# Moving and spreading a row scaling between ScalarE and GpSimd, and zero matmuls ahead of the first data, in a linear-attention and mixture-of-experts kernel

## The chip, the cores and the metric

The kernel runs on one core of a Trainium2 chip. A core has five engines with queues of their own, each of which starts its instructions in order: TensorE (PE, matrix products; the trace lists its weight loads apart, as PEld), VectorE (DVE), ScalarE (ACT), GpSimd (POOL) and SyncE (SP, here only for issuing transfers). They wait for each other by semaphores. SBUF is the on-chip memory of 128 partitions, PSUM the eight banks that TensorE writes its products to, and DMA engines move data from and to HBM. The metric is the device time of one launch in microseconds.

## What is computed

The reference runs a linear attention with an exponential feature map over 8 batches and 8 heads of 576 positions, then routes the 4608 resulting rows of 512 values to 8 experts with weights P found by 8 rounds of row and column normalisation:

```python
def phi(x):
    proj = np.einsum('bhsd,df->bhsf', x, w_phi)
    proj = proj - np.max(np.abs(proj), axis=-1, keepdims=True)
    return np.concatenate([np.exp(proj), np.exp(-proj)], axis=-1)
...
num = np.einsum('bhsf,bhfd->bhsd', q_p, kv)
den = np.einsum('bhsf,bhf->bhs', q_p, z)[..., None] + 1e-06
...
for e in range(E):
    h = np.maximum(x @ w1[e], 0.0)
    ye = h @ w2[e]
    out += P[:, e:e + 1] * ye
```

Each expert has a product up from 512 to 1024 and a product down to 512. The output of expert e is scaled row by row with column e of P and added up.

## The kernel before

**Order.** The program does not give instructions to the engines as it goes. It first writes a list of operations (`plan.op`, through the helpers `pe`, `act`, `dve`, `pool` and `dma`), each with its engine, an estimated duration, what it reads and writes (keys), and the buffers that it takes. `Plan.schedule` then plays the list through: at each step it takes the operation that can start earliest, on whichever engine, and among several that can start at the same time the one written first. That gives every engine's order. On the chip only the order within an engine and the true dependences remain; the estimated times do not. Estimates that matter below: TensorE columns / 2400 + 0.0025 us, ScalarE columns / 1200 + 0.09 us, VectorE columns / 960 + 0.09 us, GpSimd 0.00164 us for each unit of its given size + 0.17 us; a result reaches another engine 0.22 to 0.32 us after that. Operations marked `shared` (all of `pool`, and VectorE's sums through `sub`) are planned so that only one of them runs at a time on the two engines together.

**Start.** Transfers of the first k, q and v tiles go out on SP's queue (`load_qk`, `load_v`, lines 811 to 828), w_phi in two halves on the queues of ScalarE and GpSimd (line 813). VectorE meanwhile fills small tiles (lines 818, 833, 835) and casts w_phi (line 820). The first matrix work is the transposes of k and q (line 545, `pair_a`), whose results VectorE and ScalarE copy out (lines 549, 553); then come products with w_phi (recorded at line 468, the helper `mm`), maxima on VectorE (line 460) and exponentials on ScalarE (line 464).

**Attention and the first expert.** The string `order` at line 873 lists the steps of attention by hand, with the first expert's products (`up0`, `down0`) for the first groups among them. Rows come in nine groups g of 512. `down0` puts the first expert's output unscaled into `acc[g]`, a float32 tile of 128 x 4 x 512, since P isn't known yet: ScalarE copies two of the four row blocks (line 795), VectorE the others (line 802). `routing` computes P in a chain of small VectorE operations and TensorE products (lines 929 to 945) while the first expert's last groups are multiplied. P ends with line 945.

**Experts 1 to 7.** For each expert, `load_w` transfers the weights from GpSimd's queue (line 362), `sums_w` builds eight sums of weight quarters on VectorE (line 986), and nine loops over g run the seven products of Strassen's method in both directions, interleaved by the string `ORDER` (line 1282): the up products of group g (`up7`) with the down products of the group before it (`down7`, the entries X1, Y1, Z1, X2, X3, Z2, X4). All these products are recorded at line 1078. In `up7` ScalarE copies a bank out to U (line 1106) or applies the relu (line 1115), and VectorE adds U to another bank (line 1110). A bank is added to further only after it has been copied. In `down7` VectorE first makes four sums of hT (line 986). The results go to `acc[g]` in two ways: `read2` scales a bank with P on ScalarE (line 1230) and adds it on GpSimd (line 1233); `read` does both on VectorE (line 1218).

**The scaling of the first expert's output.** When `down7` is called for expert 1, it writes four operations for its group, ahead of the group's products (lines 1238 to 1243): `acc[g]` times column 0 of P, in place, on ScalarE. They need P, the first expert's output in `acc[g]`, and nothing else; so all 36 can start as soon as P and those outputs are there. Both kinds of additions to `acc[g]` in expert 1 wait for them.

Of the kernel before, what the change touches and what calls it, by code (L numbers as in the profile page):

```python
# [12 lines left out]
ALU = mybir.AluOpType  # L13
ACT = mybir.ActivationFunctionType
# [214 lines left out]
def kernel(  # L229
# [11 lines left out]
    nc = tc.nc  # L241
# [3 lines left out]
    N, DD = out.shape  # L245
# [22 lines left out]
    xT = const.tile([128, NP, N], BF16, name="xT")  # L268
    L = const.tile([128, NT, E], FP32, name="L")
    P = const.tile([128, NT, E], FP32, name="P")  # L270

    NA = 5
    acc = [accp.tile([128, 4, DD], FP32, name=f"acc{g}", tag=f"acc{g}") for g in range(NA)]
# [17 lines left out]
    def pe(cols, fn, r=(), w=(), takes=()):  # L291
        plan.op("PE", max(cols / 2400.0 + 0.0025, 0.032), 0.32, fn, r, w, takes)

    def act(el, fn, r=(), w=()):
        plan.op("ACT", el / 1200.0 + 0.09, 0.22, fn, r, w)

    def dve(el, fn, r=(), w=(), shared=False):
        plan.op("DVE", el / 960.0 + 0.09, 0.22, fn, r, w, shared=shared)

    def pool(el, fn, r=(), w=()):  # L300
        plan.op("POOL", el * 1.64e-3 + 0.17, 0.25, fn, r, w, shared=True)

    def dma(queue, nbytes, rate, fn, r=(), w=()):

        plan.op(queue, 0.8 if queue == "POOL" else 0.6, 0.0, fn, r, w, (), nbytes / rate / (125 / 100))
# [45 lines left out]
    def new(tag):  # L351
        return banks.new(int(tag[1])) if tag in ("P1", "P2") else R[tag].new()
# [29 lines left out]
    def load_qk(b, hh, nh, t, r=()):  # L382

        o = hh % 4
        keys = [o // 2] if nh == 2 else [0, 1]
        if b < 2:
            g = t["f"]
            for x, src in ((1, k), (0, q)):
                i = 2 * x + o // 2
                dma("SP", nh << 17, 268, lambda x=x, src=src, i=i: nc.sync.dma_start(  # L390
                    out=acc[g][:, i:i + nh // 2].rearrange("p a (h c) -> p (a h) c", h=2),
                    in_=src[b, hh:hh + nh, 0:SM].rearrange("h (p j) d -> p h (j d)", j=NJ)),
                    r, [("acc", g, 2 * x + n) for n in keys])
            return
        for x, src in ((1, k), (0, q)):
            dma("POOL", nh << 17, 200, lambda x=x, src=src: nc.gpsimd.dma_start(
                out=t["qk"]()[:, x, o:o + nh],
                in_=src[b, hh:hh + nh, 0:SM].rearrange("h (p j) d -> p h (j d)", j=NJ)),
                r, [(t["qk"], x, i) for i in keys])
# [25 lines left out]
    def new_half(b, i):  # L425

        t = {"T": new("qkT"), "v": new("v_m")}
        if b < 2:
            return {"f": 4 - 2 * b - i, **t}
        return {"qk": new("qk"), **t}  # L430
# [36 lines left out]
    def mm(out_, lhsT, rhs, start, stop):  # L467
        nc.tensor.matmul(out_, lhsT=lhsT, rhs=rhs, start=start, stop=stop)  # L468
# [310 lines left out]
    def akey(g):  # L779
        return ["late"] * (g >= NA) + ["P"] * (g >= 9)  # L780
# [27 lines left out]
    for b in range(2):  # L808
        for i in range(2):
            halves[b, i] = new_half(b, i)  # L810
    load_qk(0, 0, 2, halves[0, 0])
    for i, (queue, eng) in enumerate((("ACT", nc.scalar), ("POOL", nc.gpsimd))):
        dma(queue, 1 << 15, 100, lambda i=i, eng=eng: eng.dma_start(
            out=wphi_f[64 * i:64 * i + 64, :], in_=w_phi), w=[f"wphi_f{i}"])
# [4 lines left out]
    for i in range(2):  # L819
        dve(64, lambda i=i: nc.vector.tensor_copy(  # L820
            out=wphi2[64 * i:64 * i + 64, i, :], in_=wphi_f[64 * i:64 * i + 64, :]),
# [4 lines left out]
    for h0 in (4, 6):  # L826
# [3 lines left out]
        out=wgate, in_=moe_w_gate.rearrange("(c p) e -> p c e", p=128)), w=["wgate"])  # L830
    for i in range(2):
        for x in range(2):
            dve(300, lambda i=i, x=x: nc.vector.memset(vrd[i][x], 0.0),
                w=[("vrd", i, x, h, *y) for h in range(2) for y in ((), (1,))])
# [338 lines left out]
    def down7(e, g, hT, B7):  # L1173


        def a(i, j):
            return lambda: hT[j]()[:, :, 256 * i:256 * i + 256]

        def hk(i, j):
            return [(hT[j], fp, i) for fp in range(2)]  # L1180

        late, seen = akey(g), set()
        S = [new("S") for _ in range(4)]
        S01 = dve
        sub(dve, 1024, lambda: S[2](), a(0, 0), a(1, 0), ALU.subtract, hk(0, 0) + hk(1, 0),
            [S[2]])
        sub(S01, 1024, lambda: S[0](), a(1, 0), a(1, 1), ALU.add, hk(1, 0) + hk(1, 1), [S[0]])
        sub(S01, 1024, lambda: S[1](), lambda: S[0](), a(0, 0), ALU.subtract,
            [S[0]] + hk(0, 0), [S[1]])
        sub(dve, 1024, lambda: S[3](), a(0, 1), lambda: S[1](), ALU.subtract,  # L1190
            [S[1]] + hk(0, 1), [S[3]])

        def prod(bank, lhs, y, r, first, more=()):
            f, r2 = B7[y]
            product(bank, lambda k, i: lhs()[:, k, 128 * i:128 * i + 128],
                    lambda k: f()[:, k, :], 4, r + r2 + (["P"] if e else late) + list(more), first)

        def start(bank, i, j):

            out_ = acc_part(g, i, j)  # L1200
            w = [("acc", g, 2 * i + n, j) for n in range(2)]
            if (i, j) in seen:
                dve(500, lambda: nc.vector.tensor_tensor(
                    out=out_(), in0=bank().rearrange("p (a b) -> p a b", a=2), in1=out_(),
                    op=ALU.add), [bank] + late, w)
            else:
                act(512, lambda: nc.scalar.copy(
                    out=out_(), in_=bank().rearrange("p (a b) -> p a b", a=2)),
                    [bank] + late, w)
            seen.add((i, j))  # L1210

        def read(bank, i, j):

            if e == 0:
                return start(bank, i, j)
            for n in range(2):
                ts = 2 * i + n
                dve(330, lambda n=n, ts=ts: nc.vector.scalar_tensor_tensor(  # L1218
                    out=acc[g][:, ts, 256 * j:256 * j + 256],
                    in0=bank()[:, 256 * n:256 * n + 256], scalar=P[:, 4 * g + ts, e:e + 1],  # L1220
                    in1=acc[g][:, ts, 256 * j:256 * j + 256], op0=ALU.mult, op1=ALU.add),
                    [bank, "P"], [("acc", g, ts, j)])

        def read2(bank, i, j):

            if e == 0:
                return start(bank, i, j)
            u = new("V")
            for n in range(2):
                act(390, lambda n=n: nc.scalar.activation(  # L1230
                    out=u()[:, n, :], in_=bank()[:, 256 * n:256 * n + 256], func=ACT.Copy,
                    bias=0.0, scale=P[:, 4 * g + 2 * i + n, e:e + 1]), [bank, "P"], [(u, n)])
            pool(670, lambda: nc.gpsimd.tensor_tensor(  # L1233
                out=acc[g][:, 2 * i:2 * i + 2, 256 * j:256 * j + 256],
                in0=acc[g][:, 2 * i:2 * i + 2, 256 * j:256 * j + 256], in1=u(), op=ALU.add),
                [(u, 0), (u, 1)], [("acc", g, 2 * i + n, j) for n in range(2)])

        if e == 1 and g < 9:
            for ts in range(4):
                act(512, lambda ts=ts: nc.scalar.activation(  # L1240
                    out=acc[g][:, ts, :], in_=acc[g][:, ts, :], func=ACT.Copy, bias=0.0,
                    scale=P[:, 4 * g + ts, 0:1]), ["P", ("acc", g, ts)] + akey(g),
                    [("acc", g, ts, j) for j in range(2)])
        x, y, z = new("P1"), new("P1"), new("P1")

        def X1():
            prod(x, a(0, 0), "11", hk(0, 0), True, S[1:3])
            read2(x, 0, 0)

        def Y1():  # L1250
            prod(y, a(0, 1), "21", hk(0, 1), True)
            read2(y, 0, 0)

        def Z1():
            prod(z, lambda: S[0](), "t1", [S[0]], True, S[3:4])
            read2(z, 1, 1)

        def X2():
            prod(x, lambda: S[1](), "t2", [S[1]], False)
            read(x, 0, 1)  # L1260

        def X3():
            prod(x, lambda: S[2](), "t3", [S[2]], False)
            read2(x, 1, 1)

        def Z2():
            prod(z, lambda: S[3](), "22", [S[3]], False)
            read(z, 0, 1)

        def X4():  # L1270
            prod(x, a(1, 1), "t4", hk(1, 1), False)
            read(x, 1, 0)

        def stores():
            if e == E - 1:
                for ts in range(4):
                    store(g, ts)

        return {"out": stores, "X1": X1, "Y1": Y1, "Z1": Z1, "X2": X2, "X3": X3, "Z2": Z2, "X4": X4}
# [56 lines left out]
```

## Time and profile before

| | |
|---|---|
| median of 3 runs | 1036.67 us (1035.63 to 1037.01) |
| the profiled execution | 1036.16 us |
| its span in the trace | 1034.4 us |
| attention with the first expert's first groups | 0 to about 206 us |
| the rest of the first expert, and the routing | about 206 to 254 us |
| experts 1 to 7 | about 253 to 1034 us |
| the 36 scalings of line 1240 on ScalarE | 24.3 us busy, first 243.4, last 278.3 us |

In the listings of single pieces of work, a row gives the start in microseconds from the span's start, the duration, the engine, the line, the operation, what it writes and reads, the shape, and how many such instructions in a row were merged (x2). In brackets stands how long the engine had stood idle before, and what released it. A listing of one line or tile gives durations in nanoseconds as minimum/median/maximum, and the first and last start. Matmuls are pipelined: the record of a 256-column product is 273 ns long while the next one starts some 109 ns after it, so a merged row is longer than its products' share of time by that tail.

### The profile page before, as it was taken

The page shows a single profiled execution, that of the slowest core. Times are in us where ns is not written, and L with a number is a line of the kernel's source. Part 1 is how long each engine was busy: PE and PEld are TensorE (multiplying, and loading weights), DVE is VectorE, ACT ScalarE, POOL GpSimd, SP SyncE. Part 2 cuts the span into 40 slices and gives each one's busy share as a digit, 9 for nine tenths or more (in the row PEclk, how much of TensorE's full clock was granted, in tenths as well). Part 3 has the DMA queues.
Part 4 walks back from the last instruction along what each step waited for, and adds up shares of the span by engine and source line. Part 5 has one row for each costly group of instructions (what it writes and reads, how often), then busy time and mean ns, then how long its engine had stood idle before and what let it go on. Part 6 is the DMA issues. An engine that isn't in the chain of part 4 may idle for free.

```text
span 1034.4 us, 24481 instructions
## 1 busy us (share of the span) xinstructions
PE 1013.8 (98%) x9476; PEld 843.0 (81%) x9512; DVE 823.7 (80%) x1626; ACT 710.9 (69%) x1569; POOL 462.8 (45%) x534
## 2 busy tenths in 40 slices
PE   7899999999999999999999999999999999999998
PEld 5666666645788888888888888888888888888886
DVE  7999998987677788778777787788677877786775
ACT  7999999837966666666666656666666566666653
POOL 5877675400243443434443444434444433334442
PEclk9999999999999999999999999999999999999999
DMA  9998996085311161115211341134111611114333
GB/s 261 175 172 145 174 162 103 2 206 140 83 42 52 46 120 41 42 46 100 73 44 50 82 83 42 42 83 92 33 52 44 131 43 42 42 51 124 123 123 123
DMA packets 105237, 93.93 MB, mean 91 GB/s; under 512 B 45392, under 2 KB 80272, under 8 KB 105120
## 3 DMA queue, kind: packets, MB, share of 16 engines
q1 hardware_dynamic: 71360, 68.44, 24.3%
q0 software_dynamic: 33680, 23.90, 16.5%
q8 instruction: 74, 1.21, 0.5%
q14 instruction: 43, 0.35, 0.1%
q10 hardware_dynamic: 80, 0.03, 0.0%
HBM read 94.98 MB, written 14.16 MB: 106 GB/s over the span
## 4 chain that ended last, share of the span: by engine, by line
PE 92%; ACT 4%; DVE 3%; issue 1%; DMA 0%; DVEq 0%; POOLq 0%
PE P L1078 73%; PE P L468 17%; ACT acc L1240 2%; PE P L667 1%; DVE m L460 1%; ACT k L464 1%; PE P L706 1%; ACT q L464 0%; DMA wphi_f<-in_w_phi_dram 0%; DVE xb L687 0%; ACT U L1106 0%; DVE P L679 0%; PE P L672 0%; DVE S L986 0%; DVE m_r L460 0%
## 5 line engine op out<-in xcount | busy, mean ns | idle before, releaser
L1233 POOL TENSOR_TENSOR acc<-acc,V 128x512 f32<-128x512 f32 x248 | 316.1, 1281 | 440.5 <-ACT V L1230 437.6
L1110 DVE CUSTOM_DVE_ANT_0 hT<-P,U 128x512 bf16<-128x512 f32 x378 | 255.1, 687 | 105.9 <-ACT U L1106 56.7
L1106 ACT COPY U<-P 128x512 f32<-128x512 f32 x378 | 217.9, 590 | 139.0 <-PE P L1078 131.0
L1230 ACT ACTIVATE V<-P 128x256 f32<-128x256 f32 x496 | 205.6, 474 | 124.4 <-PE P L1078 119.2
L1218 DVE SCALAR_TENSOR_TENSOR acc<-P,acc 128x256 f32<-128x256 f32 x372 | 160.0, 478 | 73.7 <-PE P L1078 71.6
L1078 PEld LDWEIGHTS <-w 128*128 128x128 bf16 x2016 | 197.2, 98 | 25.2 <-issue 2.0
L1078 PEld LDWEIGHTS <-S 128*128 128x128 bf16 x1984 | 194.2, 98 | 22.4
L1078 PEld LDWEIGHTS <-T 128*128 128x128 bf16 x1512 | 147.9, 98 | 19.7 <-issue 2.5
L1078 PEld LDWEIGHTS <-hT 128*128 128x128 bf16 x1488 | 145.5, 98 | 17.1 <-DVE hT L1110 0.3
L1078 PE MATMUL P<-X,w 128*128 128x256 bf16 x1008 | 154.9, 273 | 0.4 <-ACT U L1106 0.4
L1078 PE MATMUL P<-xT,w 128*128 128x256 bf16 x1008 | 152.5, 273 | 0.9 <-ACT acc L795 0.5
L1078 PE MATMUL P<-X,T 128*128 128x256 bf16 x1008 | 148.6, 273 | 1.5 <-ACT U L1106 1.5
L1078 PE MATMUL P<-w,hT 128*128 128x256 bf16 x992 | 143.4, 273 | 0.0
L1078 PE MATMUL P<-T,S 128*128 128x256 bf16 x1056 | 136.3, 273 | 0.0
L1078 PE MATMUL P<-w,S 128*128 128x256 bf16 x928 | 126.5, 273 | 0.0
L460 DVE TENSOR_REDUCE m<-P 128x4 f32<-128x512 f32 x128 | 83.7, 679 | 3.4 <-PE P L468 2.1
L593 POOL TENSOR_TENSOR v<-v_m,em 128x512 bf16<-128x512 f32 x64 | 67.0, 1046 | 43.1 <-ACT em L464 39.0
L986 DVE TENSOR_TENSOR S<-hT 128x1024 bf16<-128x1024 bf16 x124 | 83.4, 709 | 0.3 <-ACT hT L1115 0.3
L1115 ACT ACTIVATE hT<-P 128x512 bf16<-128x512 f32 x126 | 74.2, 604 | 12.4 <-PE P L1078 11.9
L468 PE MATMUL P<-w,hT 128*128 128x512 bf16 x303 | 77.1, 379 | 0.9 <-DVE m L460 0.2
L1078 PE MATMUL P<-xT,T 128*128 128x256 bf16 x504 | 76.0, 273 | 0.3
L468 PE MATMUL P<-xT,w 128*128 128x512 bf16 x271 | 71.4, 379 | 1.0 <-ACT q L464 0.3
(95 smaller groups left out, 1096.5 us busy)
## 6 DMA issues: line engine op xcount, KB each, us to landing
X<-xd SPq DMA_DIRECT2D x126, 256.0 KB, 2.6
w<-in_moe_w_dram POOLq DMA_DIRECT2D x14, 1024.0 KB, 10.1
v_m<-in_v_dram SPq DMA_DIRECT2D x14, 512.0 KB, 5.2
out_dram<-acc SPq DMA_DIRECT2D x14, 512.0 KB, 2.7
xd<-S SPq DMA_DIRECT2D x18, 256.0 KB, 2.4
qk<-in_k_dram POOLq DMA_DIRECT2D x12, 256.0 KB, 5.5
qk<-in_q_dram POOLq DMA_DIRECT2D x12, 256.0 KB, 6.5
w<-in_moe_w_dram POOLq DMA_DIRECT2D x8, 256.0 KB, 7.7
```

Of the source, the lines that this page charges most:

```text
L460: dve(el, lambda: nc.vector.tensor_reduce(out=dst(), in_=src(), axis=AX.X, op=ALU.max, apply_absolute_value=True), r, w)
L468: nc.tensor.matmul(out_, lhsT=lhsT, rhs=rhs, start=start, stop=stop)
L593: pool(512, lambda y=y, em=em: nc.gpsimd.tensor_tensor(out=s["v"][y]()[:, :, 0:D], in0=t["v"]()[:, h0:h0 + 2].rearrange("p a (b c) -> p (a ...
L986: lambda: f.tensor_tensor(out=out_(), in0=x(), in1=y(), op=op), r, w, **kw)
L1078: pe(256, lambda i=i, k=k, z=z: nc.tensor.matmul(bank()[:, 256 * i:256 * i + 256], lhsT=lhs(k, i), rhs=rhs(k), start=first and z, stop=k = ...
L1106: act(512, lambda: nc.scalar.copy(out=u[fp][n]().rearrange("p a b -> p (a b)"), in_=x[fp]()), [x[fp]], [u[fp][n]])
L1110: dve(500, lambda: nc.vector._custom_dve(ADD_SAT, out=out_(fp, i, j), in0=bank[fp]().rearrange("p (a b) -> p a b", a=2), in1=u[fp][n](), s ...
L1115: act(512, lambda: nc.scalar.activation(out=out_(fp, i, j), in_=x[fp]().rearrange("p (a b) -> p a b", a=2), func=ACT.Relu, bias=0.0, scale ...
L1218: dve(330, lambda n=n, ts=ts: nc.vector.scalar_tensor_tensor(out=acc[g][:, ts, 256 * j:256 * j + 256], in0=bank()[:, 256 * n:256 * n + 256 ...
L1230: act(390, lambda n=n: nc.scalar.activation(out=u()[:, n, :], in_=bank()[:, 256 * n:256 * n + 256], func=ACT.Copy, bias=0.0, scale=P[:, 4 ...
L1233: pool(670, lambda: nc.gpsimd.tensor_tensor(out=acc[g][:, 2 * i:2 * i + 2, 256 * j:256 * j + 256], in0=acc[g][:, 2 * i:2 * i + 2, 256 * j: ...
L1240: act(512, lambda ts=ts: nc.scalar.activation(out=acc[g][:, ts, :], in_=acc[g][:, ts, :], func=ACT.Copy, bias=0.0, scale=P[:, 4 * g + ts, ...
```

## The change

```diff
     load_qk(0, 0, 2, halves[0, 0])
+    dve(128, lambda: nc.vector.memset(xT[:, 0, 0:512], 0.0), w=[("xT", 0, 0)])
+    pz = new("P1")
+    for i in range(6):
+        pe(1024, lambda: mm(pz(), xT[:, 0, 0:128], xT[:, 0, 0:512], True, True),
+           [("xT", 0, 0)], [pz])
...
         if e == 1 and g < 9:
             for ts in range(4):
-                act(512, lambda ts=ts: nc.scalar.activation(
-                    out=acc[g][:, ts, :], in_=acc[g][:, ts, :], func=ACT.Copy, bias=0.0,
-                    scale=P[:, 4 * g + ts, 0:1]), ["P", ("acc", g, ts)] + akey(g),
-                    [("acc", g, ts, j) for j in range(2)])
+                r = ["P", ("acc", g, ts)] + akey(g) + ([("acc", g - 2, 0, 0)] if g >= 2 else [])
+                w = [("acc", g, ts, j) for j in range(2)]
+                if g < 2:
+                    pool(670, lambda ts=ts: nc.gpsimd.tensor_tensor(
+                        out=acc[g][:, ts, :], in0=acc[g][:, ts, :],
+                        in1=P[:, 4 * g + ts, 0:1].to_broadcast([128, DD]), op=ALU.mult), r, w)
+                else:
+                    act(512, lambda ts=ts: nc.scalar.activation(
+                        out=acc[g][:, ts, :], in_=acc[g][:, ts, :], func=ACT.Copy, bias=0.0,
+                        scale=P[:, 4 * g + ts, 0:1]), r, w)
```

At the start, VectorE fills the first 512 columns of xT's first block with zeros, before its other fills, and TensorE multiplies them with themselves six times (128 x 128 by 128 x 512) into a PSUM bank that nothing reads. Each product has an estimate of 1024 columns. The real contents of that part of xT are written by attention later.

The eight scalings of groups 0 and 1 become GpSimd multiplications of two tensors, the second being a column of P read 512 times. They still need only P and the first expert's output. The 28 scalings of groups 2 to 8 stay on ScalarE, but each also waits for the last addition to row block 0, column half 0 of the group two before it that was listed by then: that is the addition after Y1 in expert 1, on GpSimd. Nothing else is changed by hand; the planner orders all operations anew.

## The prediction

> **What bounds the kernel now.** I read the page's busy shares first, then busy time by stage, because a share over 1034 us hides a stage of 20 us. In both views the columns after a stretch are busy us (and instructions) of PE, weight loads, DVE, ACT and POOL, then granted clock and DMA.
>
> ```profile
> PE 1013.8 (98%) x9476; PEld 843.0 (81%) x9512; DVE 823.7 (80%) x1626; ACT 710.9 (69%) x1569; POOL 462.8 (45%) x534
> ...
> 253.00:270.00 17.00, 14.00 (x113) 10.63 (x112) 10.60 (x16) 17.00 (x32) 1.53 (x2) 1.00 0.52 96
> 270.00:287.00 17.00, 17.00 (x158) 15.18 (x156) 12.28 (x23) 14.51 (x30) 6.97 (x6) 1.00 0.22 57
> 270.00:280.00 10.00, 10.00 (x94) 8.90 (x92) 7.20 (x14) 10.00 (x21) 4.44 (x4) 1.00 0.20 54
> 310.00:350.00 40.00, 40.00 (x369) 35.84 (x368) 28.93 (x52) 24.50 (x53) 17.88 (x15) 1.00 0.15 43
> ```
>
> TensorE sets the end: it is full from 270 on. One stage is different: from 253 to 270 TensorE has holes and ScalarE none (17.00 of 17). What ScalarE does there, and what TensorE waits for:
>
> ```profile
> 243.45 1.33 ACT L1240 ACTIVATE acc<-acc,P 128x512 f32<-128x512 f32 x2 [1.07 <-DVE P L945]
> 252.11 3.78 ACT L1240 ACTIVATE acc<-acc,P 128x512 f32<-128x512 f32 x6
> 255.79 0.59 ACT L795 ACTIVATE acc<-P 128x512 f32<-128x512 f32 x1
> 263.15 3.81 ACT L1240 ACTIVATE acc<-acc,P 128x512 f32<-128x512 f32 x6
> 266.82 0.61 ACT L1106 COPY U<-P 128x512 f32<-128x512 f32 x1
> ...
> 256.42 0.60 PE L1078 MATMUL P<-xT,w 128*128 128x256 bf16 x4 [0.52 <-ACT acc L795]
> 261.75 0.60 PE L1078 MATMUL P<-X,w 128*128 128x256 bf16 x4 [0.38 <-ACT U L1106]
> 264.68 0.60 PE L1078 MATMUL P<-xT,w 128*128 128x256 bf16 x4 [0.33 <-DVE hT L1110]
> 267.48 0.60 PE L1078 MATMUL P<-X,T 128*128 128x256 bf16 x4 [1.33 <-ACT U L1106]
> ```
>
> The scalings of line 1240 run in blocks of six ahead of the PSUM copies that TensorE needs: the copy at 266.82 starts as the block of 263.15 ends, and TensorE has stood for 1.33 us. The four quoted waits make 2.56 of the stage's 17 - 14.00 = 3.0 idle us. The idle number is too small, since a matmul's record is longer than its pace. So I count the matmuls of line 1078 alone (columns: PE, weight loads, clock, DMA):
>
> ```profile
> 253.00:270.00 17.00, 13.17 (x107) 10.32 (x108) 1.00 0.52 96
> 270.00:287.00 17.00, 17.00 (x158) 15.18 (x156) 1.00 0.22 57
> ...
> 253.35 0.27 PE L1078 MATMUL P<-xT,w 128*128 128x256 bf16 x1
> 253.46 0.81 PE L468 MATMUL P<-w,hT 128*128 128x512 bf16 x3
> 254.10 0.49 PE L1078 MATMUL P<-xT,w 128*128 128x256 bf16 x3
> ```
>
> At the full pace 107 matmuls take 107 x 17 / 158 = 11.5 us. The last products of the first expert take the time before the first of them at 253.35 and from 253.46 to 254.10, together 1.0 us. So 17 - 11.5 - 1.0 = 4.5 us are lost in this stage. That is the most that taking work off ScalarE can give here.
>
> **The scalings taken from ScalarE.** Before, all 36 are ready when P is, at 243.4, and ScalarE fills every opening with them, so what it does for TensorE comes late by the scalings ahead of it. Each occupies it for 3.78 / 6 = 0.63 us. Their share of ScalarE's time (the second number is their busy time, records overlapping a little):
>
> ```profile
> 243.00:268.00 25.00, 19.05 (x29) 1.00 0.66 129
> ```
>
> 29 of the 36, 19 of 25 us. After the change none of the 29 is on ScalarE there: groups 0 and 1 go to GpSimd, and each later group waits for the last addition to rows of the group two before it, which comes a loop or more after the first down products. The copies and activations then run when their products end. How much of the 4.5 returns? Not all: in this stage group 0's products have no second product stream to fill the steps from product to copy to product, and its down products wait for sums on VectorE. Between 4.5 (all) and 0 (another engine just as late) I take two thirds, 3.0 us, because nearly every wait named above ends at ScalarE, and the one on hT is itself fed by its copies.
>
> **The eight on GpSimd.** They are two-input operations of 512 columns; the nearest rows are these:
>
> ```profile
> L593 POOL TENSOR_TENSOR v<-v_m,em x64: 1035/1046/1086, 10.0 to 196.0; 128x512 bf16<-128x512 f32 x64
> L1233 POOL TENSOR_TENSOR acc<-acc,V x248: 1258/1269/1793, 269.4 to 1021.6; 128x512 f32<-128x512 f32 x124
> ...
> 245.63 0.75 POOL L362 DMA_DIRECT2D w<-in_moe_w_dram  x1 [37.88 <-PE P L468]
> 254.57 0.89 POOL L362 DMA_DIRECT2D w<-in_moe_w_dram  x1 [8.18 <-PE P L468]
> 269.35 1.27 POOL L1233 TENSOR_TENSOR acc<-acc,V 128x512 f32<-128x512 f32 x1 [13.90 <-ACT V L1230]
> ```
>
> Line 593 also has a broadcast second input, line 1233 the float32 output; I take 1.05 to 1.27 us each, 8.4 to 10.2 in all. GpSimd is idle from 243 to 269 but for two weight-load issues. The first user of a scaled row there is the addition at 269.35, so even 10.2 us from 243.4 is done by 254, with 15 us to spare. The load of 245.63 can slip behind one scaling (1.3 us at most by the planner's order); it is for the expert after this one, but one VectorE row hangs on it, next fence. What GpSimd takes from VectorE is the real price. An overlap of the two, and the sums that will meet the scalings:
>
> ```profile
> 398.09 1.26 POOL L1233 TENSOR_TENSOR acc<-acc,V 128x512 f32<-128x512 f32 x1 [0.53 <-ACT V L1230]
> 398.15 1.74 DVE L986 TENSOR_TENSOR S<-hT 128x1024 bf16<-128x1024 bf16 x1
> ...
> L986 DVE TENSOR_TENSOR S<-hT x124: 674/683/1751, 263.3 to 1008.3; 128x1024 bf16<-128x1024 bf16 x124
> ...
> 244.60 1.29 DVE L986 TENSOR_TENSOR T<-w 128x1024 bf16<-128x1024 bf16 x2
> 249.43 1.28 DVE L986 TENSOR_TENSOR T<-w,T 128x1024 bf16<-128x1024 bf16 x2
> 254.08 0.69 DVE L986 TENSOR_TENSOR T<-w 128x1024 bf16<-128x1024 bf16 x1 [1.11 <-DMA w<-in_moe_w_dram]
> ```
>
> A sum of 0.68 us that met a GpSimd addition took 1.74: it stood 1.06 us, to the end of the other. The planner knows this (both kinds are marked as sharing a port) and will deal the eight scalings out among the eight sums of expert 1's weights, which now run from 244.6 to 250.7. In a strict alternation they end at 244.6 + 8 x (0.6 + 1.27), about 259.6. The four sums of w1, which come first and which the up products need, end at 244.6 + 4 x 1.87 = 252.1, still ahead of their first product at 253.35. The four of w2 are needed for down products, which begin near 263. So the delay is covered, with 1 us of margin at its narrowest; were that gone, each further meeting costs up to 1.06. This is part of why I take 3.0 and not 4.5. The Trainium skill says the same of the two engines ("SBUF — State Buffer", "SBUF: two separate sides": whoever starts first holds the shared pair for its whole instruction and the other blocks), and the two rows at 398 agree; it speaks against moving work to GpSimd beside a dense run of sums.
>
> **The 28 spread out.** A loop of one group has 112 of these matmuls, 112 x 17 / 158 = 12.1 us. ScalarE works 24.5 of 40 in the steady stretch, 7.4 of 12.1; four scalings more make 9.8, 81%. From 270 to 280 it is at 100% and TensorE full all the same, so I cost the load at nothing. The new wait is another thing: ScalarE is in order, and the copies queued behind a scaling that waits for GpSimd's addition are what TensorE and VectorE want. From below the wait costs nothing (GpSimd is idle half of the time). From above it is one addition of 1.27 us for each of seven groups, 8.9 us. I take 0.3, near the lower end: the scaling is planned behind the end of that addition, and the group it serves is multiplied only a loop later.
>
> **The zeros.** They come first on TensorE, and a memset of 512 columns comes first on VectorE. The start:
>
> ```profile
> 1.05 2.14 DVE L833 MEMSET vrd<- 128x520 bf16 x4
> 3.58 2.13 PE L545 MATMUL P<-identf,acc 128*128 128x128 f32 x8 [3.58 <-DMA acc<-in_k_dram]
> 3.76 0.22 DVE L820 CAST wphi<-wphi_f 64x128 bf16<-64x128 f32 x1 [0.42 <-DMA wphi_f<-in_w_phi_dram]
> 5.14 0.22 DVE L820 CAST wphi<-wphi_f 64x128 bf16<-64x128 f32 x1 [1.16 <-DMA wphi_f<-in_w_phi_dram]
> 6.15 1.05 PE P L468 x4
> 7.22 2.06 ACT k L464 x4
> 7.83 1.06 PE L468 MATMUL P<-qkT,wphi 128*128 128x512 bf16 x2
> 11.34 0.60 PE L468 MATMUL P<-wphi,qkT 128*128 128x256 bf16 x4
> 20.02 0.30 PE L545 MATMUL P<-identf,acc 128*128 128x128 f32 x1 [0.46 <-DMA acc<-in_q_dram]
> ```
>
> The memset is 0.49 at most (one of the four of line 833, of 520 columns); VectorE waits 0.42 and 1.16 for w_phi soon after, which swallows it. Four matmuls that take 1.05 us at 6.15 take 0.60 at 11.34, so TensorE starts at half its pace. Two of 512 columns took 1.06 at 7.83, so six zeros take at most 3.2 us, from 1.5 at the latest (1.05 + 0.49) to 4.7, and k's transposes, half of the 2.13 at 3.58, end by 5.8. They are needed when w_phi has landed and been cast, 5.14 + 0.22 = 5.4: a loss of 0.4 at most, none if the zeros end by 4.3. If TensorE is fast by 6.15, the chain (the rows at 6.15 and 7.22 are from it) is 1.05 - 0.60 = 0.45 us shorter. But at 20.02 TensorE, in order, waits for a transfer of q that the zeros do not speed up, and most of any gain ends in that wait. Between -0.45 and +0.4 I take -0.1. The Trainium skill ("TensorE: Matmul & The Clock Gate", "Part 1: The HAM clock gate") gives some 3.4 us of sustained activity to reach the full clock, in a window that runs free of the kernel; by that alone the zeros would fall short or not by chance, and the sum would move by 0.45 or not at all. The order of attention should not change: by the planner's costs the zeros end at 0.44 + 6 x 0.43 = 3.0, before its due time of the first k (3.4).
>
> **Sum.** The profiled execution took 1036.16 us (span 1034.4 and 1.8 around it), 0.5 below the median of the runs, 1036.67. 1036.16 - 3.0 + 0.3 - 0.1 = 1033.4; with runs a little above the profile I say 1033.5.
>
> **Rivals.** A: VectorE takes ScalarE's place. It is busy 10.60 of 17 in the stage, so 6.4 are free; eight waits of 1.06 are 8.5, 2.1 over. The sums of expert 1 and group 0's sums of hT then come late, and 3.0 shrinks by 2.1 or more: 1035.5, and up to 1036.7 if each wait stands on the path. For it: the row at 398. Against: the planner keeps the two apart, and VectorE's other work can run under a scaling.
>
> B, slower: the in-order wait of the spread scalings. ScalarE reaches the scaling of group g before the addition of g - 2 is done, in each of groups 2 to 8, and stands up to 1.27 us with copies behind it. 8.9 - 3.0 - 0.1 = 5.8 more at most: 1042; from half a microsecond in each group (3.5 in all) it undoes the gain. For it: strict order and a cross-engine wait in seven loops. Against: TensorE kept full with ScalarE at 100%.
>
> C: the change gives the whole of the stage and the start, 4.5 + 0.45: 1031.2. D: it doesn't do what it says: the zeros leave TensorE's pace as it is, and the scalings of groups 2 and 3, due in the loops from about 265 on, sit ahead of the copies of those loops as the block of 263.15 does now. Half of the 3.0 stays: 1036.16 - 1.5 + 0.3 = 1035.0.
>
> **How the numbers follow.** Forecast 0.54 (its own range 1031.9 to 1034.6), A and D together 0.25, B 0.15, C 0.06. About 0.2%, 2.1 us, is what a measurement of this kernel can tell from no change. Below 1034.6, 2.1 under the median, lie the forecast and C: faster 0.60. A and D lie between, and B up to 1038.7, that is up to 0.8 us in each of the seven groups (0.05): same 0.30. The rest of B is slower: 0.10. The range 1031 to 1037.3 leaves out most of B and a little of C.
>
> **What would show it.** Right: from 253 to 270 ScalarE below 17.00, TensorE's matmuls of line 1078 near 140 in place of 107, no wait for U over 0.5; GpSimd busy from 243.4 to about 256; four matmuls at 6.15 in under 0.8. Wrong: VectorE's sums at 1.7 us there and TensorE waiting for hT (A), ScalarE's scalings with idle time before them that ends at the GpSimd addition and TensorE short of full between 280 and 370 (B), or a TensorE stage after 400 that has lost its 100%, which no step above allows.

## The result and the profile after

| | median | range | runs |
|---|---|---|---|
| before | 1037.01 us | 1035.63 to 1038.63 | 9 |
| after | 1039.70 us | 1039.00 to 1040.67 | 9 |

The ratio is 1.0027, 95% interval 1.0018 to 1.0037: the change makes the kernel 2.7 us slower. The profiled execution took 1039.43 us, 3.3 more than the one of before. In the changed kernel the lines behind the first edit are 5 higher: the products of experts 1 to 7 are at line 1083, the sums at 991, the GpSimd scalings at 1248.

Busy time by stage (us and instructions of TensorE, weight loads, VectorE, ScalarE, GpSimd, then clock and DMA). The first row is the kernel before, the others are the kernel after:

```profile
243.00:253.00 10.00, 9.91 (x46) 4.47 (x46) 7.88 (x15) 9.55 (x17) 0.75 (x1) 1.00 0.77 160
243.00:253.00 10.00, 7.79 (x37) 3.42 (x35) 10.00 (x9) 2.39 (x4) 8.21 (x9) 1.00 0.75 164
253.00:270.00 17.00, 13.59 (x91) 9.25 (x90) 10.72 (x17) 5.64 (x10) 1.72 (x2) 0.80 0.41 70
270.00:287.00 17.00, 17.00 (x158) 15.24 (x156) 13.85 (x25) 13.21 (x27) 6.12 (x5) 1.00 0.27 73
287.00:380.00 93.00, 93.00 (x854) 83.33 (x853) 72.35 (x129) 70.69 (x147) 41.28 (x34) 1.00 0.22 56
```

ScalarE is free, as forecast: 5.64 of 17 in place of 17.00. But from 243 to 253 VectorE is busy for the whole ten microseconds with nine instructions (before: 7.88 with fifteen), GpSimd for 8.2, and TensorE has holes; and the clock of the next stage is 0.80. The instructions of VectorE, then GpSimd, then TensorE in that stretch:

```profile
245.13 1.28 DVE L991 TENSOR_TENSOR T<-w 128x1024 bf16<-128x1024 bf16 x2
246.34 7.98 DVE L991 TENSOR_TENSOR w<-w 128x1024 bf16<-128x1024 bf16 x1
254.85 0.68 DVE L991 TENSOR_TENSOR T<-w 128x1024 bf16<-128x1024 bf16 x1
255.45 0.68 DVE L802 COPY acc<-P 128x512 f32<-128x512 f32 x1
...
243.78 1.15 POOL L1248 TENSOR_TENSOR acc<-acc,P 128x512 f32<-128x512 f32 x1 [35.75 <-DVE P L950]
245.91 0.81 POOL L362 DMA_DIRECT2D w<-in_moe_w_dram  x1 [0.98 <-PE P L468]
246.75 7.02 POOL L1248 TENSOR_TENSOR acc<-acc,P 128x512 f32<-128x512 f32 x7
...
245.45 5.34 PE L468 MATMUL P<-w,hT 128*128 128x512 bf16 x24
256.18 4.86 PE L468 MATMUL P<-w,hT 128*128 128x512 bf16 x13 [5.38 <-DVE acc L802]
260.88 0.27 PE L1083 MATMUL P<-xT,w 128*128 128x256 bf16 x1
```

One sum, which takes 0.68 us elsewhere, stands for 7.98. It ends 0.55 us after the last of seven scalings that GpSimd runs one behind the other from 246.75 to 253.77. Behind it in VectorE's queue waits the copy of line 802, at 255.45, which empties a PSUM bank of the first expert. TensorE needs that bank and stands for 5.38 us. Then it is slow as well: 13 products take 4.86 us. The clock (the number before the last two) over that time:

```profile
253.00:254.00 1.00, 0.00 (x0) 0.00 (x0) 1.00 (x1) 0.00 (x0) 0.77 (x1) 0.61 0.45 82
254.00:255.00 1.00, 0.00 (x0) 0.00 (x0) 1.00 (x3) 0.00 (x0) 0.00 (x0) 0.50 0.01 2
259.00:260.00 1.00, 1.00 (x4) 0.32 (x3) 0.21 (x1) 0.00 (x0) 0.00 (x0) 0.50 0.00 0
260.00:261.00 1.00, 1.00 (x7) 0.52 (x6) 1.00 (x2) 0.00 (x0) 0.00 (x0) 0.98 0.00 0
```

It falls to half some 2.4 us after TensorE's last product (its records end at 250.79; 0.61 in the slice from 253 is full clock up to about 253.2) and is back near 260, 3.8 us after the work resumes. Neither time is fixed: in e2 and e4 below, which have the same stall, the clock falls 2.2 and 4.2 us after the last product and is back 3.6 and 5.3 us after the work resumes, worked out in the same way from their slices (0.66 from 252 to 253 in e2, 0.52 from 255 to 256 in e4). Once the clock is back, TensorE hardly stands again: it is full from 270 on. Its products of experts 1 to 7 alone, after:

```profile
253.00:270.00 17.00, 8.41 (x75) 7.34 (x75) 0.80 0.41 70
270.00:287.00 17.00, 17.00 (x158) 15.24 (x156) 1.00 0.27 73
```

75 by 270 where there were 107: 32 x 17 / 158 = 3.4 us behind, close to the 3.3 between the two profiled executions. The account: the first of these products starts at 260.88 in place of 253.35, 7.5 us later, of which 5.4 are the wait, 1.9 the slow clock (4.86 less the 2.97 of the same 13 products at full clock, third run below), and the rest P, which is ready 0.3 later. Some 4.1 of the 7.5 come back by 270, because the stage, once begun, now loses next to nothing.

### The profile page after: what moved, and what is told of

It is laid out like the page before. It is cut to its first block, busy times and chain, and to the rows that moved or that the text cites. A ratio compares the mean times of both kernels' runs of the same rounds, so it can differ in the third digit from the quotient of the medians.

```text
span 1037.7 us, 24546 instructions
## 1 busy us (share of the span) xinstructions
PE 1016.4 (98%) x9518; PEld 842.6 (81%) x9518; DVE 828.5 (80%) x1627; ACT 706.1 (68%) x1561; POOL 473.1 (46%) x542
## 4 chain that ended last, share of the span: by engine, by line
PE 94%; DVE 3%; SPq 1%; DMA 1%; ACT 0%; issue 0%; POOL 0%; DVEq 0%
PE P L1083 74%; PE P L468 18%; PE P L667 1%; DMA acc<-in_q_dram 1%; DVE w L991 1%; PE P L706 1%; DVE m L460 1%; SPq L390 0%; PE P L672 0%; ACT q L464 0%; SPq L446 0%; DVE xb L687 0%; DVE P L679 0%; SPq L404 0%; DVE m_r L460 0%
## 5 line engine op out<-in xcount | busy, mean ns | idle before, releaser
L468 PE MATMUL P<-w,hT 128*128 128x512 bf16 x320 | 81.5, 386 | 5.6 <-DVE acc L802 5.4
L468 PE MATMUL P<-xT,w 128*128 128x512 bf16 x288 | 74.7, 379 | 0.3 <-ACT q L464 0.3
```

## Experiments

Theory: the seven GpSimd scalings hold up a sum, the sum the copies behind it, these TensorE, and the pause its clock. Rivals: the zeros cost the time; the 28 spread scalings do; the planner's new order does. "Before" is the kernel before on the same chip, 1036.7 to 1037.0 in all four groups of runs.

| run | edit, against the kernel after | median, us | ratio to before, 95% |
|---|---|---|---|
| e1 | zeros alone, scalings as before | 1036.71 | 1.0002 (0.9993 to 1.0010) |
| e2 | scalings alone, no zeros | 1039.41 | 1.0029 (1.0017 to 1.0041) |
| e3 | GpSimd scalings planned behind the sums | 1035.75 | 0.9994 (0.9985 to 1.0003) |
| e4 | one memset ahead of each scaling | 1040.15 | 1.0036 (1.0024 to 1.0049) |
| e5 | nothing on GpSimd | 1034.97 | 0.9978 (0.9969 to 0.9987) |
| e6 | as e3, held on the chip too | 1034.67 | 0.9981 (0.9972 to 0.9990) |
| e7 | two copies of line 802 on ScalarE | 1033.45 | 0.9967 (0.9955 to 0.9979) |
| e8 | group 0 alone on GpSimd | 1037.21 | 1.0002 (0.9993 to 1.0010) |
| e9 | e6 and e7 together | 1035.64 | 0.9990 (0.9981 to 0.9999) |
| e10 | e5 and e7 together | 1034.39 | 0.9978 (0.9969 to 0.9987) |
| e11 | eight memsets ahead of each scaling | 1032.65 | 0.9960 (0.9947 to 0.9974) |
| e12 | e7 without the zeros | 1033.42 | 0.9967 (0.9955 to 0.9980) |
| e13 | two memsets | 1032.91 | 0.9958 (0.9942 to 0.9975) |
| e14 | four memsets | 1032.39 | 0.9959 (0.9944 to 0.9974) |

The times of five runs missed the ranges expected of them: e3, e5, e8 and e9 came out 1.75, 0.5, 0.2 and 1.1 us above, e11 0.35 below. The kernels with the tile `gap` (e4, e6, e9, e11, e13, e14) have the lines behind it one higher again.

### The two halves of the change (e1, e2)

> The kernel before with the six matmuls of zeros and their memset alone. Theory (the loss is made by the scalings on GpSimd, not by the zeros): within 0.1% of before, 1036.5 to 1038; TensorE is fast by 6.0 and the first exponentials start about 0.6 us sooner (6.6 in place of 7.2), but at the transfer of q near 20 us the lead is gone, and P is ready within 0.4 us of before's 243.4. Rival (the zeros cost time, by pushing the transposes or the transfers): 1039 or more with the stage from 253 to 270 as before.

> The changed kernel without the zeros. Theory: as slow as the changed kernel, 1039 to 1040, with a sum of about 8 us on VectorE behind seven GpSimd scalings, and TensorE standing 5 us for a copy of line 802 near 251 to 256 and then at half clock. Rival (zeros): 1036 or less.

The zeros alone change nothing that can be measured, the scalings alone cost all of it. The start of the kernel after shows where the zeros' lead ends (first rows TensorE and ScalarE, then two of TensorE's waits):

```profile
1.19 2.74 PE L468 MATMUL P<-xT 128*128 128x512 bf16 x6 [1.19 <-DVE xT L812]
5.98 1.05 PE L468 MATMUL P<-wphi,qkT 128*128 128x256 bf16 x8 [0.77 <-DVE qkT L549]
6.62 2.07 ACT L464 ACTIVATE k<-P 128x512 bf16<-128x512 f32 x4 [0.79 <-PE P L468]
18.13 1.09 PE L545 MATMUL P<-identf,acc 128*128 128x128 f32 x8 [1.09 <-DMA acc<-in_k_dram]
20.31 0.30 PE L545 MATMUL P<-identf,acc 128*128 128x128 f32 x1 [0.52 <-DMA acc<-in_q_dram]
```

Eight products at 5.98 take 1.05 us where they took 1.89, and the exponentials begin at 6.62 in place of 7.22. By 18 us TensorE waits for k twice as long as before (1.09 against 0.52), and at 20 again for q, in a row that starts 0.29 us later than before's at 20.02. Nothing is left of the lead. (The clock column reads 1.00 from 1 to 12 us in both kernels, so the pace is read off the durations.) e12 asks the same without the stall in the way: it is e7 (below) less the six matmuls of zeros and their memset.

> The kernel with the last group's copies on ScalarE and the run of scalings on GpSimd, without the zeros. Theory (the zeros' lead ends at the transfers near 20 us): the same as with them, 1032.9 to 1034. Rival (the zeros gain or cost 0.4 us or more, hidden until now by the stall): outside of that.

With and without zeros: 1033.45 and 1033.42. In the single profiled executions P is ready 0.5 to 0.7 us later with zeros in all three pairs (e1 against before, which e1's expectation put at 0.4 at most; after against e2; e7 against e12). The medians show no such cost, and its cause stays open.

### Scalings away from the sums (e3, e6)

```diff
-                    pool(670, ..., op=ALU.mult), r, w)
+                    pool(670, ..., op=ALU.mult), r + B7["t4"][1], w + ["scaled"])
...
-        late = ["late"] + (["P"] if e == 1 else [])
+        late = ["late"] + (["P"] if e == 1 else []) + (["scaled"] if e == 2 else [])
```

> The changed kernel with the eight GpSimd scalings held until the eight sums of expert 1's weights are done, and the sums of expert 2's weights held until the scalings are done, so that no sum meets a run of scalings. Theory: no sum of 8 us, no wait of TensorE of more than 1 us between 243 and 270, clock 1.00 there; the stage loses at most 1 us of its matmuls, against 4.5 in before: 1032 to 1034. Rival (it is the spread of the other 28, or the new order, that costs): 1037 or more. Rival (GpSimd beside VectorE is harmless and only TensorE's clock fell for another reason): clock below 0.9 in the stage again.

The stall is nearly gone, but two scalings still ran among the sums. Three rows of e3, VectorE, GpSimd, TensorE (this execution's start ran 3 us late, so only its intervals are read):

```profile
248.95 3.80 DVE L991 TENSOR_TENSOR w<-w 128x1024 bf16<-128x1024 bf16 x2
249.54 2.04 POOL L1248 TENSOR_TENSOR acc<-acc,P 128x512 f32<-128x512 f32 x2
254.60 2.97 PE L468 MATMUL P<-w,hT 128*128 128x512 bf16 x13 [0.95 <-DVE acc L802]
```

The key that I added orders the operations in the plan only. The scalings do not read the sum, so the chip has nothing to wait for. GpSimd went on when its queue let it. Two scalings in a row made TensorE wait 0.95 us, and the clock stayed full: the 13 products take 2.97. In e6 GpSimd first copies eight columns of the last sum, a true dependence:

```diff
+                if g == ts == 0:
+                    pool(4, lambda: nc.gpsimd.tensor_copy(out=gap, in_=B7["t4"][0]()[:, 0, 0:8]),
+                         B7["t4"][1], [("acc", 0, n) for n in range(4)])
```

> The kernel that holds the scalings until the sums of expert 1's weights are done, now with a read that makes GpSimd wait for the last sum on the chip too (in the run before this the order was only planned, and two scalings ran among the sums: one sum of 3.2 us and a wait of TensorE of 0.95 us). Theory: all eight scalings after 250.5, every sum of weights under 0.8 us, no wait of TensorE for a copy of line 802; about 1 us under the run before it, 1033.5 to 1035.5. Rival (the sums were not what delayed the copies): no change from 1035.8.

```profile
251.45 0.19 POOL L1249 CAST gap<-T 128x8 f32<-128x8 bf16 x1 [4.40 <-DVE T L992]
251.60 2.03 POOL L1252 TENSOR_TENSOR acc<-acc,P 128x512 f32<-128x512 f32 x2
...
245.84 8.15 PE L469 MATMUL P<-w,hT 128*128 128x512 bf16 x37
```

In e6 the scalings start behind the last sum and TensorE runs the first expert's last 37 products in one go. As expected, 1 us under e3.

### The length of the run, and what queues behind the sum (e8, e7)

> The changed kernel with group 0 on GpSimd and group 1 on ScalarE: half the run. Theory (a sum stands for the whole of the run that it meets, TensorE waits for what the banks do not cover, and the clock falls only after some 2.5 us without work): a sum of 3 to 4 us, a wait of TensorE of 1 to 2 us, clock 1.00: 1034 to 1037. Rival (the loss is the clock's and comes with any stall): clock below 0.9 in the stage and 1038 or more.

> The changed kernel with the last group's two copies of line 802 on ScalarE, which is idle there, so that they do not queue behind the blocked sum. Theory: the sum still stands for about 8 us, but TensorE no longer waits 5.4 us for a copy; it works on to about 254 and then waits for the sums themselves, which end near 255, so that its wait is under 2 us and the clock stays at 1.00: 1033 to 1036. Rival (TensorE waits for the sums in any case): a wait over 4 us and 1038 or more.

The edit of e7 is one condition in `down0`, which puts the last group's two copies on the idle ScalarE:

```diff
-            if ts % 2:
+            if ts % 2 or g == 8:
```

VectorE and TensorE of e8, then of e7:

```profile
246.73 4.61 DVE L991 TENSOR_TENSOR w<-w 128x1024 bf16<-128x1024 bf16 x2
252.59 2.96 PE L468 MATMUL P<-w,hT 128*128 128x512 bf16 x13 [1.41 <-DVE acc L802]
```

```profile
247.32 8.59 DVE L991 TENSOR_TENSOR w<-w 128x1024 bf16<-128x1024 bf16 x2
246.43 8.15 PE L468 MATMUL P<-w,hT 128*128 128x512 bf16 x37
258.97 0.60 PE L1083 MATMUL P<-X,w 128*128 128x256 bf16 x4 [0.68 <-DVE hT L1115]
```

Runs of two, three and seven scalings made TensorE wait 0.95, 1.41 and 5.38 us, and the clock fell only with the last. In e7 the sum stands as long as in the kernel after, yet the first expert's last 37 products run in one go, and the time is 3.5 us under before. So the sums themselves were hardly urgent (0.68 us goes to an addition for hT that stood behind them); the copies behind them were.

### The spread alone (e5, e10, e9)

> The changed kernel with the scalings of groups 0 and 1 on ScalarE too; GpSimd scales nothing, the other 28 stay spread, the zeros stay. Theory (the spread frees ScalarE and is right, the loss is the run on GpSimd): no sum over 1.8 us, clock 1.00, no wait of TensorE over 0.6 us from 243 to 270, loops of groups 2 to 8 full: 1032.5 to 1034.5. Rival (the spread scalings cost as much as the stage gives, by ScalarE waiting in order for GpSimd's additions): 1036 to 1038, with TensorE waiting for U between 280 and 380.

> The last group's two copies on ScalarE and all scalings on ScalarE, 28 of them spread; nothing on GpSimd. Theory: as the spread alone, 1034 to 1035.5, because with no blocked sum the copies on VectorE are not late. Rival (the copies' place itself gains): under 1034.

> Both cures together: the last group's two copies on ScalarE, and the eight GpSimd scalings after the last sum of expert 1's weights, on the chip too. Theory (what is left in the stage is under 1 us in each of the two alone): no blocked sum, no wait over 0.7 us; 1032.5 to 1034.5. Rival (the two remove the same stall, and the rest is the planner's order): no better than the better of the two, 1033.5 to 1035.

With all scalings on ScalarE, 28 of them spread (e5), the kernel beats before by 2 us. So spreading alone pays, though less than it does together with GpSimd's eight where these hold up no copy (e7, e11, e13, e14). A wait that the kernel after does not have takes 0.8 us of it. VectorE, GpSimd and TensorE of e5:

```profile
354.63 1.67 DVE L991 TENSOR_TENSOR w<-w 128x1024 bf16<-128x1024 bf16 x1
356.22 0.68 DVE L1115 CUSTOM_DVE_ANT_0 hT<-P,U 128x512 bf16<-128x512 f32 x1
354.48 2.94 POOL L1238 TENSOR_TENSOR acc<-acc,V 128x512 f32<-128x512 f32 x2 [5.73 <-ACT V L1235]
356.95 0.60 PE L1083 MATMUL P<-xT,T 128*128 128x256 bf16 x4 [0.76 <-DVE hT L1115]
```

This is the same effect in small. A sum meets one of GpSimd's additions and takes 1.67 us in place of 0.68; the addition for hT that TensorE needs stands behind that sum, with no idle time of VectorE between them. e3, e6, e8, e9 and e10 have this wait too (0.76 or 0.77 us), the kernels with 93.00 of 93 from 287 to 380 (after, e7, e11 to e14) do not.

e10 gains nothing clear over e5, as expected. e9 missed both expectations: it is slower than e6 and e7. TensorE there starts 843 products from 287 to 380 where the kernel after has 854, and waits 0.93 us for ScalarE at 264. The planner made another order; which choice of it costs what stays open. Since it orders each kernel anew, differences of a microsecond or two between these cures can come from that alone.

### Why the sum stands through the whole run (e4, e11, e13, e14)

```diff
+                        nc.gpsimd.memset(gap, 0.0)
                         nc.gpsimd.tensor_tensor(
                             out=acc[g][:, ts, :], in0=acc[g][:, ts, :],
```

The memset, of 128x8 elements that nothing reads, stands once in e4 and two, four and eight times in e13, e14 and e11.

> The changed kernel with one GpSimd memset of 8 columns, which reads nothing, ahead of each of the eight scalings. Theory a (GpSimd keeps the shared port from one reading instruction to the next when they stand back to back, and a gap lets VectorE in): the sums and the scalings take turns, no sum longer than 1.8 us, the stall of 5.4 us is gone and the time is 1033 to 1036. Theory b (GpSimd's queue wins each time whatever stands between): a sum of 8 us or more again, 1039 to 1041.

> The changed kernel with eight memsets of 8 columns in place of one ahead of each scaling, about 0.5 to 0.8 us in which GpSimd reads nothing. Theory (VectorE gets its turn once GpSimd leaves the port free for long enough; a gap of 0.06 us was too short): the sums go through one by one between the scalings, none longer than 1.8 us, the wait of 5 us for line 802 gone: 1033 to 1036. Rival (nothing on GpSimd's queue lets VectorE in before the run is over): a sum of 11 us or more and 1042 or more.

> The changed kernel with two memsets of 8 columns ahead of each scaling, some 0.2 us without a read. Theory c1 (VectorE takes the port as soon as GpSimd has one whole instruction between that does not read, and one memset failed because its span overlaps the next scaling's start): sums and scalings take turns, no sum over 1.8 us, 1032 to 1034. Theory c2 (VectorE needs a longer free stretch, near the length of its own sum): a sum of 8 us or more, 1039 or more.

> Four memsets, some 0.5 to 0.6 us. Theory c1: turns, no sum over 1.8 us, 1032 to 1034. Theory c2 (the stretch must be longer still, 0.6 us or more): a sum of 8 us or more and 1039 or more; if two fail and four do not, the length lies between.

GpSimd and VectorE of e4, then of e13:

```profile
246.41 8.28 DVE L992 TENSOR_TENSOR w<-w 128x1024 bf16<-128x1024 bf16 x1
246.80 0.12 POOL L1250 MEMSET gap<- 128x8 f32 x1
246.87 1.05 POOL L1251 TENSOR_TENSOR acc<-acc,P 128x512 f32<-128x512 f32 x1
247.85 0.11 POOL L1250 MEMSET gap<- 128x8 f32 x1
247.91 1.04 POOL L1251 TENSOR_TENSOR acc<-acc,P 128x512 f32<-128x512 f32 x1
```

```profile
247.17 1.28 DVE L992 TENSOR_TENSOR w<-w 128x1024 bf16<-128x1024 bf16 x2
248.38 1.52 DVE L992 TENSOR_TENSOR T<-w 128x1024 bf16<-128x1024 bf16 x1
247.56 0.29 POOL L1251 MEMSET gap<- 128x8 f32 x2
247.80 1.55 POOL L1252 TENSOR_TENSOR acc<-acc,P 128x512 f32<-128x512 f32 x1
249.30 0.26 POOL L1251 MEMSET gap<- 128x8 f32 x2
249.51 1.29 POOL L1252 TENSOR_TENSOR acc<-acc,P 128x512 f32<-128x512 f32 x1
```

With one memset the next scaling starts 0.06 to 0.07 us after the memset's start, and the sum stands for 8.28 us. With two, 0.21 to 0.24 us lie between, and the two engines take turns: no sum there over 1.52 us, and some scalings now wait for VectorE (1.29 and 1.55 in place of 1.04). Four and eight memsets give the same time. So no long stretch is needed, but more than one memset with its 0.06 us; whether the time or the number of instructions counts is not separated here. The weight load that GpSimd issues ahead of the run is not what holds the sum: in e13 that issue lasts from 246.75 to 247.57, and the sum that starts at 247.17 beside it takes its normal time. e13, e14 and e11 are the fastest kernels of this study, 3.9 to 4.4 us under before, with memsets that compute nothing. The products of experts 1 to 7 in e11 (line 1084 there):

```profile
253.00:270.00 17.00, 15.64 (x141) 13.83 (x142) 1.00 0.53 103
270.00:287.00 17.00, 17.00 (x159) 15.24 (x156) 1.00 0.24 63
```

141 by 270, 34 more than before: 3.7 us ahead.

## Why the prediction was wrong

**The step that failed** is the sentence "In a strict alternation they end at ... about 259.6", with "the planner knows this ... and will deal the eight scalings out among the eight sums". Two things were wrong in it. The planner's dealing is a plan: GpSimd and VectorE have no dependence on each other there, so after the weight load at 245.91 GpSimd ran its remaining seven scalings at once (e3 against e6 shows the difference between planned and held). And the engines did not take turns: the row at 398 showed one GpSimd addition with nothing behind it. From it I took 1.06 us for each meeting; back to back, one meeting cost 7.3 us (7.98 - 0.68). e13 is what I had described, and its time, 1032.9, is close to my 1033.5. The copies that were late in the kernel after stand among the sums there too, and TensorE does not wait for them.

**What the price was read off.** I put the sums' deadline at their own users, the up products at 253 and the down products at 263. The first user to be late was another: the copies of line 802 behind the sums in VectorE's queue, needed at 250.8 by products of the first expert. The kernel before already had them among the sums:

```profile
248.82 0.69 DVE L802 COPY acc<-P 128x512 f32<-128x512 f32 x1 [0.53 <-PE P L468]
252.28 0.69 DVE L802 COPY acc<-P 128x512 f32<-128x512 f32 x1 [1.56 <-PE P L468]
```

The first of these is the one that ran at 255.45 after the change. e7, with the last group's two copies elsewhere and the blocked sum as it was, has none of the loss. Rival A had the right engine, but the same price of 1.06 and the same late users. Its sum was also wrong: it took VectorE's free time from 253 to 270, while the sums run from 244.6, where VectorE was busy for 7.88 of 10; and eight waits of 1.06 that all stand on the path would have given 1033.4 + 8.5 = 1041.9, not 1036.7. The clock's fall, 1.9 us more, stood in no step.

**ScalarE's part** was right in its mechanism and too small. I took 3.0 of 4.5 us. e11 gains 3.7 by 270 although its P is ready 0.5 us later (243.45 against 242.96), together 4.2.

**The durations on GpSimd** were just under the range I took, 1.05 to 1.27: 1.03 us each, 1.15 for the first.

**The 28 spread scalings** were costed at 0.3 and cost nothing in the kernel after: TensorE is full from 270 to 380, with 93.00 of 93. Rival B did not occur: none of ScalarE's waits from 243 to 382 there is that of a scaling for a GpSimd addition. The 0.8 us wait of e5 comes from a blocked sum, not from a scaling.

**The zeros** were costed at -0.1; e1 and e12 show none that can be measured, and the lead ends at the transfers near 20 us as argued.

The Trainium skill ("SBUF — State Buffer", "SBUF: two separate sides") speaks of a hold "for the whole instruction"; the sums at 1.5 us in e13 agree, while in the kernel after a sum was kept out through seven instructions (7.98 us), which that sentence doesn't tell. The Trainium skill ("TensorE: Matmul & The Clock Gate", "Part 1: The HAM clock gate") gives half clock after an idle window of about 3.4 us; here it came 2.2, 2.4 and 4.2 us after the last product (e2, after, e4), so the pause that TensorE can afford may be shorter than that.

## What to carry to other kernels

An order that a planner makes across engines holds on the chip only where one engine truly waits for the other; where GpSimd's two-input work stands back to back beside VectorE's two-input sums without a dependence, assume that GpSimd runs all of it first. Price a blocked instruction by what queues behind it on its engine, not by who reads its result: here moving two copies to an idle engine, or 0.2 us of non-reading work between the scalings, turned a loss of 2.7 us into a gain of 3.5 to 4. And a long pause of TensorE costs more than the pause: that of 5.4 us cost 1.9 more at half clock, those of 0.95 and 1.41 us cost nothing more.

## What had not been expected of the hardware

GpSimd kept VectorE's two-input sum out through seven scalings back to back, and a memset that starts 0.06 us ahead of each did not let it in, while two memsets with 0.21 us did. It did not hold the other way round: in e13 VectorE's sums stood back to back too, and GpSimd waited for one of them at most. Why one memset is too little stays open. The sum that stood had its record begin at 246.34, before the scaling at 246.75, so the record's start is not the moment at which it got its operands. Zeros as operands count as work for TensorE's clock: the first transposes run at about the same time with and without them (from 3.74 and 3.58), and the eight products near 6 us take 1.05 in each of after, e1 and e7, but 1.89, 1.89 and 1.53 in before, e2 and e12. The clock can also fall without one long pause: in e7 it drops near 11 us (0.98 from 10 to 11, 0.50 from 11 to 12), where TensorE had stood three times for 0.5 to 0.9 us with little work between.
